# An mLSTM layer and a feed-forward layer on one core: gate tiles of the second unit by matmul, a divided last store, and a new order of the work

## The chip, the cores and the metric

One core of one Trainium2 chip runs the whole program. Its engines are TensorE (PE in the rows, and PEld for its weight loads), VectorE (DVE), ScalarE (ACT), GpSimd (POOL) and SyncE (SP), each with an instruction queue of its own that is worked in order; 16 DMA engines move data. The metric is the time of one execution on the device in microseconds (us), less is better. "Faster" and "slower" are said of the median of several runs.

## The reference

```python
def _attn_ref(q, k, v, i_gate, f_gate, o_gate):          # all (4, 8, 768, 40), gates (4, 8, 768)
    ...
    for t in range(S):
        m_new = np.maximum(f_gate[:, :, t] + m, i_gate[:, :, t])
        f_stab = np.exp(f_gate[:, :, t] + m - m_new)
        i_stab = np.exp(i_gate[:, :, t] - m_new)
        m = m_new
        C = f_stab * C + i_stab * outer(v_t, k_t)         # shapes left out
        n = f_stab * n + i_stab * k_t
        y[:, :, t] = sigmoid(o_t) * (C @ q_t) / max(abs(n @ q_t), 1)

def _moe_ref(x, w_in, w_out):                             # x (3072, 320), w_in (320, 2048), w_out (2048, 320)
    h = x @ w_in
    g = h * np.clip(h + 3.0, 0.0, 6.0) / 6.0
    return g @ w_out
```

The recurrent layer (batch 4, 8 heads, 768 steps, head size 40) gives 3072 tokens of 320 numbers; the feed-forward layer then works on every token for itself.

## The kernel before, in words

**Tiles and stages.** The sequence is cut into six blocks of 128 steps; a block of one batch entry is a chunk, so there are 24 chunks. Seven units follow each other: units 0 and 1 hold two chunks each, the others four (`UL`, line 23). Each unit is worked for two halves of the heads ("quad" 0 and 1). Within a chunk the recurrence is written as matrix products: a chunk's load `st` (q and k) and `nat` (k and v) come in, `xya` (lines 479, 489) makes the scores S and the state's product K, the gate tile `gw` weighs the scores (line 419), `C` is the running state (lines 452, 455), and the outputs B (lines 500 to 512) go to `ht` (lines 464, 469). Groups `xya` on TensorE hold B of one chunk together with S and K of the next.

**Gate tiles.** The gates of a block are scanned on VectorE into `f_s` and `i_s` (lines 274 to 286). For unit 0 (`GBT = 2`: two halves of the heads of one unit) TensorE makes the tile `gb` in PSUM from the mask, `f_s` and `i_s` with a selector `sel` (lines 378, 381, 384), and ScalarE takes its exponential into `gw` (line 388). For all later units `f_s` is stored to DRAM (`gsc`, line 285), loaded back in rows that repeat over 64 partitions (line 397), and then mask and `cT` are added (lines 401, 406) and the exponential is taken (lines 414 or 416; in four parts, with `cT` as bias, where the addition is left out).

**End of a unit's first layer.** `fin` divides and multiplies with the output gate: line 593 (needs `ht`), 595, 596, 597 and 598 into `on`; `turn` transposes `on` on TensorE (`xa`, line 613), and ScalarE and VectorE split it into a high part `xh` (line 621) and a low part `xl` (line 623).

**Second layer.** `h` is made for 128 of the 2048 inner columns at a time: eight matmuls (line 738) into one of two PSUM banks. ScalarE and VectorE make `g` of it (lines 755, 757; for unit 0 it is called `gv`), and from unit 1 on `g` is split into `gh` (lines 205 and 207 are the copy helper) and `gl` (line 768). `acc` sums the output (line 781 for unit 0, lines 784 to 786 later); `evac` copies `acc` to `ob` and stores it (lines 800, 803).

**Weights.** Both weight matrices come as eight slices each of 640 KB, `rawi` and `rawo` (line 640), over three buffers, as 64-bit numbers. ScalarE (lines 648, 653, 658) and VectorE (lines 663, 664, 674 or 669) make 32-bit floats of them, and `whi`, `wlo`, `wtl` (lines 205 or 207, 692, 693, 695) are their high and low parts. All sixteen slices are done in the first 90 us or so, beside units 0 and 1.

**Order.** A table `ORDER` written into the kernel lists every step once, with the letter of the engine that does it (p TensorE, d VectorE, a ScalarE, g GpSimd, q SyncE's queue) and the buffer it takes; "F" is a filler matmul on `pw` (line 232), which computes nothing that is used. The steps are issued in this order, so each engine's queue is the table with the other engines' steps left out. Steps whose data are not there hold up what is behind them on their engine.

Of the kernel before, what the change touches and what calls it, by code (L numbers as in the profile page):

```python
# [142 lines left out]
def mlstm_moe_kernel(ctx: ExitStack, tc: tile.TileContext, ig, fg, qkd, natd, ond, w_in, w_out, ident_d, out, dump=None):  # L143
# [92 lines left out]
    def f_setup():  # L236
# [5 lines left out]
        for h in range(2):  # L242
            cs_ = slice(h * Q, h * Q + Q)
            nc.gpsimd.affine_select(sel[:, :, cs_], sel[:, :, cs_], pattern=[[-16, 2], [-1, 6], [0, Q]], compare_op=ALU.is_equal, fill=0.0, base=-8 * h, channel_multiplier=1)
# [677 lines left out]
```

## Time and profile before

| | |
|---|---|
| median of 3 runs | 465.71 us (465.06 to 465.93) |
| time of the profiled execution | 464.87 us |
| its span, first to last instruction | 463.2 us |
| TensorE busy | 449.1 us, 97% of the span |
| VectorE, ScalarE, GpSimd busy | 298.8, 215.8, 122.4 us |
| granted TensorE clock, mean | 0.996 of full speed |
| read from HBM, written | 44.53 MB, 4.03 MB |

How to read it: a busy share is a mean over stages. In the first 80 us nearly all engines are busy; from then on TensorE alone is. Idle time on another engine costs nothing unless TensorE waits for it. Matmuls are pipelined, and the ends of their rows are modelled; the distance from start to start tells what one takes.

### The profile page before, as it was taken

To read this page: it belongs to the slowest core of one execution; us is meant where nothing else is said; L and a number is where in the kernel's file an instruction comes from. 1 tells how busy PE (TensorE), PEld (TensorE's weight loads), DVE (VectorE), ACT (ScalarE), POOL (GpSimd) and SP (SyncE) were. 2 spreads that over 40 slices of the span, in tenths; PEclk is the share of its full clock that TensorE was granted. 3 is DMA by queue.
4 is the path that set the end of the run, shared out by engine and by line. 5 is a ranking of instruction groups with operands and counts; after the bars stand their busy time and mean duration, and the time that the engine had idled before them with its cause. 6 is when DMAs were issued, how large, how long until landed. Compare 5 with 4: busy or idle time off the path is not lost.

```text
span 463.2 us, 12600 instructions
## 1 busy us (share of the span) xinstructions
PE 449.1 (97%) x5243; PEld 388.3 (84%) x5249; DVE 298.8 (65%) x752; ACT 215.8 (47%) x482; POOL 122.4 (26%) x155
## 2 busy tenths in 40 slices
PE   8879989999999999999999999999999999999997
PEld 4547767899888888988889988988989898989896
DVE  6999999978866376856655763576555646443423
ACT  5788798777343434263343353243551232321231
POOL 3152225265311307502213134132112201020130
PEclk9989999999999999999999999999999999999999
DMA  6998887276304450244421442432322000010001
GB/s 208 281 315 265 234 258 203 59 176 169 94 20 119 119 151 4 78 142 121 115 77 44 131 139 60 108 102 89 101 69 78 1 1 1 16 57 1 1 1 57
DMA packets 24977, 49.38 MB, mean 107 GB/s; under 512 B 2840, under 2 KB 15960, under 8 KB 24920
## 3 DMA queue, kind: packets, MB, share of 16 engines
q1 hardware_dynamic: 24696, 47.89, 35.5%
q8 instruction: 41, 0.67, 0.6%
q10 hardware_dynamic: 224, 0.69, 0.5%
q14 instruction: 16, 0.13, 0.1%
HBM read 44.53 MB, written 4.03 MB: 105 GB/s over the span
## 4 chain that ended last, share of the span: by engine, by line
PE 85%; DVE 9%; ACT 2%; issue 1%; DMA 1%; SPq 0%; DVEq 0%; ACTq 0%
PE h L738 35%; PE acc L784 11%; PE acc L785 11%; PE acc L786 11%; PE xya L506 3%; PE xya L479 3%; PE pw L232 2%; PE xya L489 2%; PE xa L613 2%; PE xya L512 2%; PE acc L781 1%; DVE on L597 1%; DMA st<-in_qk_dram 1%; DVE on L598 1%; DVE gv L757 1%
## 5 line engine op out<-in xcount | busy, mean ns | idle before, releaser
L755 ACT ACTIVATE g<-h,half 128x512 f32<-128x512 f32 (+1 forms) x96 | 61.8, 651 | 128.3 <-PE h L738 92.9
L784 PE MATMUL acc<-vh,gh 128*128 128x320 f32 x352 | 111.5, 317 | 0.0
L757 DVE SCALAR_TENSOR_TENSOR g<-g,h 128x512 f32<-128x512 f32 (+1 forms) x96 | 61.2, 640 | 77.4 <-ACT g L755 77.3
L785 PE MATMUL acc<-vl,gh 128*128 128x320 f32 x352 | 108.6, 309 | 0.0
L786 PE MATMUL acc<-vh,gl 128*128 128x320 f32 x352 | 108.5, 308 | 0.0
L768 POOL TENSOR_TENSOR gl<-g,gh 128x512 fp32r<-128x512 f32 (+1 forms) x40 | 48.7, 1222 | 183.6 <-DVE gh L207 104.2
L738 PE MATMUL h<-xh,whi 128*128 128x512 f32 (+1 forms) x224 | 83.9, 375 | 2.4 <-DVE gv L757 1.7
L738 PE MATMUL h<-xh,wlo 128*128 128x512 f32 (+1 forms) x224 | 80.8, 361 | 0.0
L738 PE MATMUL h<-xl,whi 128*128 128x512 f32 (+1 forms) x224 | 80.5, 360 | 0.0
L784 PEld LDWEIGHTS acc<-vh,gh 128*128 128x128 f32 x352 | 66.0, 188 | 2.5
L785 PEld LDWEIGHTS acc<-vl,gh 128*128 128x128 f32 x352 | 66.1, 188 | 1.8
L786 PEld LDWEIGHTS acc<-vh,gl 128*128 128x128 f32 x352 | 66.0, 188 | 0.0
L738 PEld LDWEIGHTS h<-xh,whi 128*128 128x128 f32 x224 | 42.0, 187 | 11.4 <-DVE gv L757 3.7
L205 ACT CAST gh<-g 128x512 fp32r<-128x512 f32 (+1 forms) x53 | 30.0, 571 | 39.8 <-PE acc L785 19.5
L738 PEld LDWEIGHTS h<-xh,wlo 128*128 128x128 f32 x224 | 42.1, 188 | 6.9
L768 DVE TENSOR_TENSOR gl<-g,gh 128x512 fp32r<-128x512 f32 (+1 forms) x56 | 40.0, 722 | 12.2 <-ACT gh L205 10.9
L738 PEld LDWEIGHTS h<-xl,whi 128*128 128x128 f32 x224 | 42.1, 188 | 4.5
L738 PE MATMUL h<-xl,wtl 128*128 128x512 f32 (+1 forms) x112 | 40.5, 361 | 0.0
L738 PE MATMUL h<-xh,wtl 128*128 128x512 f32 (+1 forms) x112 | 40.2, 359 | 0.0
L419 DVE TENSOR_TENSOR gw<-xya,gw 128x256 f32<-128x256 f32 x48 | 20.0, 416 | 10.7 <-PE xya L489 7.4
L452 DVE SCALAR_TENSOR_TENSOR C<-C,dec,xya 128x42 f32<-128x42 f32 x100 | 20.6, 251 | 9.1 <-PE xya L489 9.0
L207 DVE CAST gh<-g 128x512 fp32r<-128x512 f32 (+1 forms) x43 | 19.3, 451 | 7.5 <-PE acc L785 6.1
(136 smaller groups left out, 683.2 us busy)
## 6 DMA issues: line engine op xcount, KB each, us to landing
st<-in_qk_dram SPq DMA_DIRECT2D x48, 280.0 KB, 4.2
nat<-in_nat_dram SPq DMA_DIRECT2D x48, 206.0 KB, 3.2
rawo<-in_w_out_dram SPq DMA_DIRECT2D x8, 640.0 KB, 7.9
gw<-gsc SPq DMA_DIRECT2D x20, 256.0 KB, 4.3
rawi<-in_w_in_dram SPq DMA_DIRECT2D x7, 640.0 KB, 8.5
out_dram<-ob SPq DMA_DIRECT2D x24, 160.0 KB, 3.0
on<-in_on_dram SPq DMA_DIRECT2D x5, 640.0 KB, 4.9
rawi<-in_w_in_dram ACTq DMA_DIRECT2D x1, 640.0 KB, 4.2
```

The lines of the kernel that those rows point to most:

```text
L205: nc.scalar.copy(dst, src)
L207: E(c).tensor_copy(dst, src)
L419: add(f"fr{nm}", "d", lambda e: nc.vector.tensor_tensor(V["gw", task][:, cp], V["xy", "S", nm][:, :, 0:128].rearrange("p c (j t) -> p j c ...
L452: nc.vector.scalar_tensor_tensor(Cn[:, j], cur[:, j], dc[:, j : j + 1], kv[:, hc, j], ALU.mult, ALU.add)
L479: nc.tensor.matmul(xy[h * Q : h * Q + Q, c, j * Q : j * Q + Q], st[rs, j, h], st[rs, j, 2 + (h != c)], start=True, stop=True)
L738: nc.tensor.matmul(hp[:, :n], w, x[:, :n], start=k == 0, stop=k == len(seq) - 1)
L755: nc.scalar.activation(V["g", nm], V["h", nm][:, :n], AF.Relu, bias=half, scale=1.0 / 6.0)
L757: add(f"gg{nm}", "d", lambda e: nc.vector.scalar_tensor_tensor(V["g", nm], V["g", nm], 1.0, V["h", nm][:, :n], ALU.min, ALU.mult), [f"re{n ...
L768: add(f"gl{nm}", "gd", lambda e: E(e).tensor_sub(V["gl", nm], V["g", nm], V["gh", nm].bitcast(F32)), [f"gh{nm}"], kind="tt", n=n, lock=1)
L784: nc.tensor.matmul(acc, gh[:, ts_], V["VH", f // 4][:, f % 4, :], start=f == 0, stop=False)
L785: nc.tensor.matmul(acc, gh[:, ts_], V["VL", p][:, f % 2, :], start=False, stop=False)
L786: nc.tensor.matmul(acc, gl[:, ts_], V["VH", f // 4][:, f % 4, :], start=False, stop=f == NF - 1)
```

## The change

Three things are changed. First, `GBT` goes from 2 to 4: the gate tiles of unit 1 too are made by TensorE from `f_s` and `i_s`. The selector `sel` has 16 rows of columns instead of 12, there are four `gw` buffers instead of three (and two `ob` instead of three), and only those blocks of `f_s` that a later unit loads are stored, so block 0 is not stored any more. Second, the last output tile of the last unit is copied and stored in two halves of 160 columns. Third, `ORDER` is another: nearly every step stands elsewhere, 248 steps are on another engine than before, and there are 47 fillers for 49. In `fin`, the first steps now wait for all chunks by name instead of the last one, which changes what the order may do and no arithmetic.

```diff
-GBT = 2
+GBT = 4
...
-SLOTS = dict(..., gw=3, ..., ob=3, rd=3)
+SLOTS = dict(..., gw=4, ..., ob=2, rd=3)
...
 ORDER = """
-1a 908a0 T F F F F 2q 3d 4d 5d F F F F F 6d 7d 9d F 909a0 912d 913d F F 910a0 107p0/0 F 0q 16d 11p0 12d 919q1 911a 914d 916d 917d 14a F F 920a1 923d
...
-    sel = early["ea"].tile([BR, 12, 128], F32, name="sel")
+    sel = early["ea"].tile([BR, 16, 128], F32, name="sel")
...
+    stored = {pair(u, cp)[0] for u in range(NU) for quad in range(2) if 2 * u + quad >= GBT for cp in range(UL[u])}
...
-        for c in range(c0, c0 + n):
+        for c in sorted(stored & set(range(c0, c0 + n))):
             add(st(k, c), "q", lambda e, c=c: nc.sync.dma_start(gsc[...], f_s[...]), [f"sf{nm}"], kb=16, rate=200)
...
-                    nc.tensor.matmul(pb[:, j], sel[:, 6 * quad + 2 * b + j], f_s[:, cl * L : cl * L + L], start=False, stop=False)
+                    nc.tensor.matmul(pb[:, j], sel[:, 8 * quad + 2 * b + j], f_s[:, cl * L : cl * L + L], start=False, stop=False)
...
-        add(f"r1{nm}", "d", r1, [f"b2{task}_{c0 + n - 1}"], get=[(f"rd{nm}", ("rd",))], kind="tiny", n=8)
+        add(f"r1{nm}", "d", r1, [f"b2{task}_{c0 + i}" for i in range(n)], get=[(f"rd{nm}", ("rd",))], kind="tiny", n=8)
...
+        parts = 2 if (u, t) == (NU - 1, UL[u] - 1) else 1
+        W = DM // parts
+        for x in range(parts):
+            cs = slice(x * W, x * W + W)
...
+            add(f"ev{nm}", "da" if x else "ad", ev, [f"m2_{u}_{NF//2-1}_{t}"] + [f"ev{u}_{t}"] * x, ...)
+            add(f"so{nm}", "qa" if x else "q", lambda e, cs=cs: Dq(e).dma_start(out[t0 : t0 + L, cs], V["ob", u, t][:, cs]), [f"ev{nm}"], kb=0.5 * W, rate=300)
```

How the table moves instructions, in three places. Lines of the changed kernel are two higher from line 259 on, and nine or so at the end.

SyncE's queue at the start of the program, before (`gsc<-f_s` is the store of the gates, `rawi` a weight slice, `st` and `nat` a chunk's loads):

```order
L273 DMA i_s<-in_ig_dram 64x128
L254 DMA ident<-in_ident_dram 128x128
L640 DMA rawi_177<-in_w_in_dram 128x1280
L285 DMA gsc<-f_s 4x8x128
L359 DMA nat_0_1_216<-in_nat_dram 128x412
L354 DMA st_0_0_218<-in_qk_dram 112x640
L359 DMA nat_0_0_220<-in_nat_dram 128x412
L397 DMA gw_0_256<-gsc 64x512
```

and now:

```order
L275 DMA i_s<-in_ig_dram 64x128
L642 DMA rawi_153<-in_w_in_dram 128x1280
L254 DMA ident<-in_ident_dram 128x128
L642 DMA rawi_204<-in_w_in_dram 128x1280
L361 DMA nat_0_0_241<-in_nat_dram 128x412
L642 DMA rawi_256<-in_w_in_dram 128x1280
L356 DMA st_0_0_270<-in_qk_dram 112x640
L361 DMA nat_0_1_301<-in_nat_dram 128x412
```

The store and the load of `gw` are gone from here; weight slices have moved forward.

TensorE's queue ahead of the transposes `xa` of unit 0, before (`pw` is the filler):

```order
L232 MATMUL pw<-ones 128x512
L613 MATMUL xa_0_0_512<-ident,on_479 128x128 x2
L613 MATMUL xa_1_0_520<-ident,on_479 128x128 x2
L613 MATMUL xa_2_0_525<-ident,on_479 128x128 x2
L232 LDWEIGHTS ones
```

and now (`gb` is a gate tile of unit 1, `xya` the sixth chunk's group, with the loads `st` and `nat` of unit 1):

```order
L383 MATMUL gb_1_1_598<-f_s,sel 128x128 x2
L386 MATMUL gb_1_1_598<-sel,i_s 64x2x64 x4
L502 LDWEIGHTS ones
L502 MATMUL xya_607<-ones 64x84
L502 LDWEIGHTS ones
L502 MATMUL xya_607<-ones 64x84
L508 MATMUL xya_607<-C_0_0_0_558,st_0_0_529 64x42 x4
L514 MATMUL xya_607<-nat_0_0_483,gw_0_292 64x42 x8
L481 MATMUL xya_607<-st_0_1_593 64x64 x8
L491 MATMUL xya_607<-nat_0_1_485 64x42 x8
L615 MATMUL xa_1_0_647<-ident,on_550 128x128 x2
```

A gate tile and the group of the sixth chunk now stand where fillers stood.

VectorE's queue from the last product `on` of unit 0 to its `xl`, before (`yi`, `yo` are weight slices in work, ISA is the addition of their parts):

```order
L597 SCALAR_TENSOR_TENSOR on_479<-on_479,ht_1_494 128x2x160
L663 TENSOR_SCALAR yi_516<-yi_516 128x640
L598 TENSOR_TENSOR on_479<-on_479,rd_1_0_508 128x2x160
L664 TENSOR_SCALAR yi_516<-yi_516 128x640
L623 TENSOR_TENSOR xl_534<-xa_0_0_512,xh_533 128x256
L674 ISA yi_516<-yi_516,lwi_528 128x1280
L370 TENSOR_TENSOR nat_0_0_542<-nat_0_0_542,wT 128x160
L623 TENSOR_TENSOR xl_534<-xa_1_0_520,xh_533 128x256
L623 TENSOR_TENSOR xl_534<-xa_2_0_525,xh_533 128x256
```

and now:

```order
L600 TENSOR_TENSOR on_550<-on_550,rd_1_0_583 128x2x160
L665 TENSOR_SCALAR yo_586<-yo_586 128x640
L671 ISA vr_643<-yo_512,lwo_527 128x1280
L697 TENSOR_TENSOR wlo<-yi_457,whi 128x2x256
L666 TENSOR_SCALAR yo_586<-yo_586 128x640
L207 COPY C_0_1_0_663<-xya_607 128x84
L694 TENSOR_TENSOR wtl<-yi_457,wtl 64x128
L695 TENSOR_TENSOR wtl<-yi_457,wtl 64x128
L625 TENSOR_TENSOR xl_655<-xa_2_0_651,xh_654 128x256
L625 TENSOR_TENSOR xl_655<-xa_0_0_657,xh_654 128x256
L625 TENSOR_TENSOR xl_655<-xa_1_0_647,xh_654 128x256
```

Seven steps, six of them on weights, now stand between that product and the first `xl`.

## Rows read from the trace of the kernel before

**Rows 1.** The page: busy time of the engines, share of the span, instructions.
```profile
PE 449.1 (97%) x5243; PEld 388.3 (84%) x5249; DVE 298.8 (65%) x752; ACT 215.8 (47%) x482; POOL 122.4 (26%) x155
```

**Rows 2.** Windows: length; busy us of PE, PEld, DVE, ACT, POOL; clock, DMA share, GB/s.
```profile
0.00:34.60 34.60, 28.98 (x385) 16.67 (x391) 28.31 (x83) 24.37 (x53) 12.00 (x23) 0.95 0.86 268
34.60:87.00 52.40, 48.66 (x618) 38.98 (x610) 49.82 (x128) 44.20 (x90) 17.40 (x21) 1.00 0.77 221
87.00:459.90 372.90, 371.45 (x4259) 332.67 (x4251) 220.71 (x542) 146.76 (x340) 93.05 (x111) 1.00 0.26 76
459.90:463.20 3.30, 0.03 (x1) 0.00 (x0) 0.00 (x0) 0.43 (x1) 0.00 (x0) 1.00 0.27 99
```

**Rows 3.** Groups by line and shape: VectorE whole, GpSimd from 31 to 81 us.
```profile
L664 DVE TENSOR_SCALAR yo<-yo 128x640 uint32<-128x640 uint32 x8 | 5.2, 648 | 0.1
...
L664 DVE TENSOR_SCALAR yi<-yi 128x640 uint32<-128x640 uint32 x8 | 3.9, 487 | 0.1
L692 DVE TENSOR_TENSOR wtl<-yi,wtl 64x128 fp32r<-64x128 f32 x8 | 3.4, 425 | 0.3
...
L693 DVE TENSOR_TENSOR wtl<-yi,wtl 64x128 fp32r<-64x128 f32 x8 | 2.3, 288 | 0.2
...
L598 DVE TENSOR_TENSOR on<-on,rd 128x320 f32<-128x320 f32 x2 | 2.1, 1046 | 0.0
...
L695 POOL TENSOR_TENSOR wlo<-yi,whi 128x512 fp32r<-128x512 f32 x4 | 5.5, 1382 | 6.4 <-DVE f_s L283 4.5 <-ACT whi L205 1.9
```

**Rows 4.** Timeline of VectorE and GpSimd: start us, us, engine, line, operation [idle before].
```profile
30.54 0.48 DVE L598 TENSOR_TENSOR on<-on,rd 128x320 f32<-128x320 f32 x1
30.94 0.49 DVE L664 TENSOR_SCALAR yi<-yi 128x640 uint32<-128x640 uint32 x1
...
33.19 0.74 DVE L623 TENSOR_TENSOR xl<-xa,xh 128x256 fp32r<-128x256 f32 x2
...
43.59 1.40 DVE L692 TENSOR_TENSOR wtl<-yi,wtl 64x128 fp32r<-64x128 f32 x1
...
43.58 1.27 POOL L695 TENSOR_TENSOR wlo<-yi,whi 128x512 fp32r<-128x512 f32 x1 [4.45 <-DVE f_s L283]
...
83.77 0.41 DVE L757 SCALAR_TENSOR_TENSOR g<-g,h 128x256 f32<-128x256 f32 x1
```

**Rows 5.** Waits of TensorE: us in total, times, longest.
```profile
PE h L738 <- DVE gv L757: 1.7, 3, 0.9
```

**Rows 6.** Timeline of TensorE.
```profile
1.26 5.30 PE L232 MATMUL pw<-ones 128*128 128x512 bf16 x12 [1.26 <-DVE tiny L179]
...
15.24 0.28 PE L378 MATMUL gb<-maskb,identb 128*128 128x256 bf16 x1
...
16.69 1.04 PE L232 MATMUL pw<-ones 128*128 128x512 bf16 x4
...
34.62 0.38 PE L738 MATMUL h<-xh,whi 128*128 128x256 f32 x1
...
85.99 0.44 PE L506 MATMUL xya<-C,st 40*64 40x42 f32 x16
...
87.07 0.39 PE L738 MATMUL h<-xh,whi 128*128 128x256 f32 x1
```

**Rows 7.** Timeline of SyncE's queue: the issues of DMAs.
```profile
2.23 0.43 SPq L640 DMA_DIRECT2D rawi<-in_w_in_dram  x1
5.63 0.75 SPq L285 DMA_DIRECT2D gsc<-f_s  x1
```

**Rows 8.** Last copy, last store, and the landing of all stores.
```profile
459.97 0.43 ACT L205 COPY ob<-acc 128x320 f32<-128x320 f32 x1 [0.45 <-PE acc L786]
460.42 0.33 SPq L803 DMA_DIRECT2D out_dram<-ob  x1
...
DMA to landing us min/median/max: 1.8/3.0/4.3
```

**Rows 9.** DMA issues on the page: count, KB each, median us from issue to landing.
```profile
st<-in_qk_dram SPq DMA_DIRECT2D x48, 280.0 KB, 4.2
```

More of the change, by code (lines that the diff above doesn't have):

```diff
@@ L243, in f_setup @@
             cs_ = slice(h * Q, h * Q + Q)
[L244 removed]
+            nc.gpsimd.affine_select(sel[:, :, cs_], sel[:, :, cs_], pattern=[[-16, 2], [-1, 8], [0, Q]], compare_op=ALU.is_equal, fill=0.0, base=-8 * h, channel_multiplier=1)
         nc.gpsimd.memset(mask, 0.0)
@@ L270, in gates @@
         gbs = [f"gb{t // 2}_{t % 2}_{cp}" for t in range(GBT) for cp in range(UL[t // 2]) if blk(pair(t // 2, cp)[0]) == k - 1]
-        sts = [st(k - 1, c) for c in range(c0 - GP[k - 1], c0)] if k else []
+        sts = [st(k - 1, c) for c in range(c0 - GP[k - 1], c0) if c in stored] if k else []
         add(f"lf{nm}", "qa", lambda e: Dq(e).dma_start(f_s[:, :w], fg[:, cols]), [f"pT{p}"] * (k > 0) + sts + gbs, kb=BR * w * 4 / 1000, rate=110)
@@ L380, in gb @@
                 for j in range(2):
[L381 removed]
+                    nc.tensor.matmul(pb[:, j], sel[:, 8 * quad + 2 * b + j], f_s[:, cl * L : cl * L + L], start=False, stop=False)
                 for h in range(2):
                     for cc in range(2):
[L384 removed]
+                        nc.tensor.matmul(pb[h * Q : h * Q + Q, :, cc], i_s[:, cl * L + cc * Q : cl * L + cc * Q + Q], sel[:, 8 * quad + 2 * b : 8 * quad + 2 * b + 2, h * Q : h * Q + Q], start=False, stop=cc == 1)
             add(f"gb{nm}", "p", gb, [f"if{g}"] + [f"gb{u}_{quad}_0"] * (cp > 0), get=[(f"gb{nm}", ("ey", "eo", "ez"))] + ([(f"gw{task}", ("gw",))] if cp == 0 else []), kind="gb")
@@ L796, in evac, with ev @@
         t0 = b * S + c * L
-        def ev(e):
-            V["ob", u, t] = P["mo"].tile([128, DM], F32, tag=f"ob{got[f'ob{u}_{t}'][1]}", name=f"ob{u}_{t}")
-            cast(e, V["ob", u, t], V["acc", u, t])
-        add(f"ev{u}_{t}", "ad", ev, [f"m2_{u}_{NF//2-1}_{t}"], get=[(f"ob{u}_{t}", ("ob",))], kind="pcp", n=DM)
-        T.free(f"acc{u}_{t}", [f"ev{u}_{t}"])
-        add(f"so{u}_{t}", "q", lambda e: nc.sync.dma_start(out[t0 : t0 + L, :], V["ob", u, t]), [f"ev{u}_{t}"], kb=164, rate=300)
-        T.free(f"ob{u}_{t}", [f"so{u}_{t}"])
+        parts = 2 if (u, t) == (NU - 1, UL[u] - 1) else 1
+        W = DM // parts
+        for x in range(parts):
+            cs = slice(x * W, x * W + W)
+            nm = f"{u}_{t}" + "b" * x
+            def ev(e, x=x, cs=cs):
+                if x == 0:
+                    V["ob", u, t] = P["mo"].tile([128, DM], F32, tag=f"ob{got[f'ob{u}_{t}'][1]}", name=f"ob{u}_{t}")
+                cast(e, V["ob", u, t][:, cs], V["acc", u, t][:, cs])
+            add(f"ev{nm}", "da" if x else "ad", ev, [f"m2_{u}_{NF//2-1}_{t}"] + [f"ev{u}_{t}"] * x, get=[(f"ob{u}_{t}", ("ob",))] if x == 0 else (), kind="pcp", n=W)
+            add(f"so{nm}", "qa" if x else "q", lambda e, cs=cs: Dq(e).dma_start(out[t0 : t0 + L, cs], V["ob", u, t][:, cs]), [f"ev{nm}"], kb=0.5 * W, rate=300)
+            T.free(f"acc{u}_{t}", [f"ev{nm}"])
+            T.free(f"ob{u}_{t}", [f"so{nm}"])
     for i in range(WS):
```

150 lines of the change are left out of this document (75 added, 75 removed).

## The prediction

> **What bounds the kernel now.** I read the page first: TensorE is busy for 449.1 of 463.2 us, so the time is TensorE's work plus what it wastes [rows 1]. The windows say where the waste lies: 5.6 us idle up to the first `h` matmul at 34.6, 3.7 us from there to 87, 1.5 us in all of 87 to 459.9, and 3.3 us behind the last matmul [rows 2]. The 49 filler matmuls on `pw`, all ahead of 34 us, are waste as well. The rest TensorE has to do in any order, so this change can move time only ahead of 87 us, in the tail, or in a few later waits. Ahead of 87 us VectorE is the tight engine: 49.82 of 52.40 us busy between 34.6 and 87, with ScalarE at 44.20 and the DMA engines at 0.77 [rows 2]. VectorE keeps its own pace only when GpSimd is quiet: the first `wtl` subtraction of a pair takes 425 ns on average and the second, of the same size, 288 [rows 3]; the one of 1.40 us at 43.59 ran beside a GpSimd `wlo` that began at 43.58 [rows 4]. TensorE's own waits agree: `h` waits for VectorE's `gv` [rows 5].
>
> The sum is made against the profiled execution: span 463.2 us, own time 464.87, which is 0.84 us under the median of 465.71. I work out a difference and put it on the median.
>
> **The change, part by part.**
>
> *Four gate tiles on TensorE.* One tile is lines 378 to 384: from 15.24 until the filler at 16.69, 1.45 us [rows 6]; four cost 5.8 us. Two fillers go, at (1.04 - 0.38) / 3 = 0.22 us each where four run on end [rows 6], 0.4 us. All of it stands ahead of the first `h` matmul, where TensorE waits or fills, so by itself it costs nothing; without that cover it would be 5.4 us.
>
> *What they replace.* Four loads of `gw` and the store of block 0 to `gsc`; on GpSimd and ScalarE mask additions, `cT` additions and exponentials in four parts. None of these engines is the tight one there, so I take no gain from the work itself. The store mattered for its place: SyncE issued a weight load at 2.23 and then held its queue for that store until 5.63 [rows 7]; now two more loads can go out without that hold. Whether it helps is a rival's matter. The wider `sel` is a third more of two fills and two selects, done while VectorE waits for the first gate rows: nothing.
>
> *VectorE up to the first `h` matmul.* By the order, 18 steps are new ahead of the last `xl` of unit 0 and 8 are gone. New: `w4` and `w5` of two output-weight slices and one `w6`, together 4 x 0.4 + 0.75; one more `wlo`, 0.6; one more `th`, 0.45; state steps of unit 1 and one `fr`, 0.9; the rest trades one slice for another. Each counts with the distance to the next start: 0.4 us from 30.54 to 30.94, where the row's own 0.48 includes the end of the pipeline [rows 4]. Net 4.3 us. The last `xl` ended at 33.93 [rows 4], so now at 38.2, and with 0.5 us for TensorE to come up the first `h` starts at 38.7 instead of 34.62 [rows 6]. TensorE's own queue is no earlier either: seventeen fillers instead of twelve precede the first gate tile, and the twelve took 5.30 us from 1.26 on, over 0.4 each [rows 6]. That is 4.1 us; but the sixth chunk's `xya` is by then done already, 1.1 us as from 85.99 to 87.07 [rows 6], which leaves 3.0.
>
> *From there to 87 us.* The place to read is the fifth `h` of unit 1, at 87.07 [rows 6]: in both orders the same TensorE work stands ahead of it, gate tiles and fillers apart. With two `h` banks it needs the third product `g` of unit 1, which VectorE ran from 83.77 to 84.18 [rows 4]: 2.9 us to spare. In the new order VectorE has 6.5 us more ahead of that product: by then the slices are even, but it has five `wlo` for two, three `whi` for one, the scans of gate group 2 and three steps of `gh` and `gl` that stood later (1.8, 0.8, 2.3, 0.8, and small ones). Two gains stand against it. GpSimd loses about 7 of its 17.4 us in this stretch [rows 2], above all three `wlo` of 1.38 [rows 3]. What GpSimd costs VectorE I take from pairs of equal work: 8 x (648 - 487) + 8 x (425 - 288) ns for the shifts and `wtl`, and 2 x (1046 - 485) ns for `on` against the quiet row at 30.54 [rows 3, 4], 3.5 us, which is 0.2 us per us of GpSimd: 1.4 us back. And of VectorE's 2.6 idle us there [rows 2] I give a half back, 1.3, since more steps are ready. That puts the product's end at 84.18 + 6.5 - 1.4 - 1.3 = 88.0, 0.9 us behind 87.07. TensorE alone would be there at 38.7 + 52.4 - 3.7 idle [rows 2] - 1.1 for the `xya` = 86.3 at the latest, so it waits. What was 3.0 us late at 38.7 is 0.9 us late here, and **that 0.9 is the whole cost of the new start**, since TensorE is full from there on. Bounds: with no slowdown and no idle left, VectorE is 5 us earlier and TensorE's 86.3 decides, less what its busy time hides of waits, -1.5 to -3; with both left whole, +2.7.
>
> *Later waits.* The 1.5 us behind 87 [rows 2] belong to the old order; a new one has its own, between -1.5 and +1.5. I take -0.4: these gone, and about 1 us of others.
>
> *The last store in halves.* Now: copy from 459.97 to 460.40, store issued at 460.42, end at 463.2, 2.7 us behind the issue; stores of this size land in 1.8 to 4.3 us [rows 8]. The second half is ready no earlier, since both copies run on ScalarE: 0.3 us each by half of 0.43 and its fixed part, the second 0.2 behind the first, 0.5 in all. It goes out by ScalarE's queue, whose issue no row near the end shows; I let it cost as much again as SyncE's 0.33 [rows 8]. Gain at most the 0.9 between 2.7 and the quickest landing, loss at most 0.4; I take -0.2, nearer to the row of this very store. The Trainium skill (DMA: Bandwidth & Descriptors, Anatomy of one DMA) speaks against a gain: it has a DMA cost a fixed 2.0 us plus its bytes over 436 GB/s, so that halving 160 KB saves an estimated 0.19 us, and the later copy takes that back: by it the tail would be 0.0 and the sum 0.2 us higher. The 2.7 us here fit it better than a time in proportion to size would.
>
> Sum: 0.9 - 0.4 - 0.2 = +0.3 us, so 466.0; I cut it to **465.9**, which is no change that a measurement of this kernel can tell (about 0.2%, 0.93 us).
>
> **The rivals.**
>
> *Faster.* VectorE is relieved by more than I count: loads start 3.4 us sooner [rows 7], so its early idle shrinks, and GpSimd no longer slows a step. Then the product of the place above is done by 85, the three waits of `h` for `gv` (1.7 us, up to 0.9 [rows 5]) end, and TensorE is 1.7 us early at 87: with tail and later waits -2.4, 463.3. For it: 3.7 us of idle to be had [rows 2]. Against it: VectorE does get more work.
>
> *Slower.* In the new order the sixth chunk's `xya` stands directly ahead of the first `xa`, so `xa` waits for that chunk's `st`. Up to it the queue holds about 8 MB: seven weight slices of 640 KB, six `st` of 280 [rows 9], seven somewhat smaller `nat`, and small ones. At the 268 GB/s of the first 34.6 us [rows 2] that has moved by 30, and it lands some 4 us later, since an `st` lands 4.2 us behind its issue [rows 9]: 34 or so. VectorE has 3 us of weight steps between its last `on` product and the first `xl`, so the wait is free until `xya` starts at 34.9; from there each us is one on the first `h`. A load at 37 puts that at 40.8, VectorE can't make 2.1 us up, and the time is 467.9. For it: DMA engines at 0.86 [rows 2]. Against it: the 3.4 us that SyncE's queue gains.
>
> *The change does little of what it says:* the loads saved are worth nothing while the DMA engines stay full; that lies inside the forecast, which takes no gain from them.
>
> **How the numbers follow.** The forecast case, within 1.2 us of 465.9, has 0.42: 0.27 of it within 0.2%, 0.06 under, 0.09 over. Faster has 0.33, slower 0.25. So faster 0.39, same 0.27, slower 0.34. Both signs hold much, so the range leaves out about a quarter of the faster case, towards its bound of -3, and a third of the slower one: 462.8 to 468.2. The forecast case alone: 464.7 to 467.1.
>
> **What would show it.** Right: the first `h` matmul at 38 to 39.5, right behind VectorE's last `xl`; the fifth `h` of unit 1 within 1.5 us of 87 and waiting for `g`; TensorE at 9 in the page's later slices; 2.4 to 2.8 us behind the last issue. Wrong: a first `h` behind 40 with `xya` waiting for `st` (slower); 86 or less at the fifth `h` of unit 1 (faster); a new wait of over 1 us behind 90, for which I have no term.

## The result: slower by 0.6%

| | before | after |
|---|---|---|
| median (19 runs of each) | 465.71 us (464.51 to 468.15) | 468.82 us (466.39 to 471.17) |
| ratio, 95% interval | | 1.0059 [1.0042, 1.0077] |
| profiled execution, own time | 464.87 us | 468.0 us |
| its span | 463.2 us | 466.3 us |
| first `h` matmul | 34.62 us | 39.64 us |
| fifth `h` of unit 1 | 87.07 us | 89.31 us |
| from there to the last matmul's end | 372.86 us | 373.66 us |
| behind the last matmul | 3.3 us | 3.3 us |
| granted TensorE clock, mean | 0.996 | 0.992 |

Slower, by more than a measurement can confuse with no change. The profiled span grew by 3.07 us: 2.24 up to the fifth `h` of unit 1, 0.8 behind it, nothing in the tail. Lines of the kernel after stand two higher than before in this stretch of the file (740 for 738).

The page's line of busy times of the kernel after, which answers to [rows 1]:

```profile
PE 454.6 (97%) x5299; PEld 394.9 (85%) x5299; DVE 294.8 (63%) x740; ACT 202.2 (43%) x440; POOL 145.6 (31%) x180
```

TensorE is busy 5.5 us longer; VectorE and ScalarE have less to do, GpSimd 23.2 us more, all of it behind the fifth `h` (118.23 for 93.05). The windows of the kernel after (columns as in [rows 2]):

```profile
0.00:39.64 39.64, 35.60 (x499) 21.92 (x500) 31.14 (x94) 29.16 (x62) 12.21 (x23) 0.96 0.88 271
39.64:89.31 49.67, 47.39 (x552) 39.93 (x552) 46.97 (x124) 37.74 (x80) 15.12 (x19) 0.97 0.71 199
56.24:59.65 3.41, 3.41 (x17) 3.41 (x17) 2.86 (x11) 3.41 (x7) 1.31 (x2) 0.50 1.07 247
89.31:462.97 373.66, 371.59 (x4249) 333.05 (x4248) 216.71 (x524) 134.84 (x298) 118.23 (x138) 1.00 0.26 75
462.97:466.30 3.33, 0.00 (x0) 0.00 (x0) 0.00 (x0) 0.49 (x2) 0.00 (x0) 0.93 0.20 61
```

The third row is a stretch at a granted clock of 0.50, the lower of the two levels (1.2 GHz), although TensorE was busy for all of its 3.41 us: its `h` matmuls started 0.21 us apart there, for 0.12 elsewhere. Just ahead of it TensorE had waited twice, 0.39 and 0.64 us. One more stretch at 0.50, at 35.8 to 39.2, lies inside the first row; the profile of before has one, at 30.7. In both places TensorE had no `h` yet. The fourth row's idle time is 2.07 us, where before had 1.5. Waits of TensorE in the kernel after (waits view: us in total, times, longest):

```profile
PE pc L312 <- ACT cTs L205: 0.8, 1, 0.8
PE h L740 <- DVE g L759: 0.8, 1, 0.8
PE pc L312 <- DVE cTs L207: 0.6, 1, 0.6
PE h L740 <- DVE gv L759: 0.6, 1, 0.6
PE acc L783 <- DVE vr L671: 0.6, 1, 0.6
...
PE gb L380 <- ACT gw L390: 0.6, 1, 0.6
...
PE xya L481 <- DMA st<-in_qk_dram: 0.2, 1, 0.2
```

The three waits of `h` for `gv` [rows 5] have become one; the waits for `cTs`, of `h` for `g` and of `gb` are new in the list, and the one for `vr` was 0.5 us in before. Where they stand, in rows picked from TensorE's timeline of the kernel after (start, busy time, line, operation, idle time before it and what ended it):

```profile
32.21 0.27 PE L380 MATMUL gb<-maskb,identb 128*128 128x256 bf16 x1 [0.56 <-ACT gw L390]
39.64 0.36 PE L740 MATMUL h<-xh,whi 128*128 128x256 f32 x1 [0.45 <-DVE xl L625]
86.17 1.34 PE L783 MATMUL acc<-vr,gv 128*128 128x320 f32 x4 [0.58 <-DVE vr L671]
89.31 0.39 PE L740 MATMUL h<-xh,whi 128*128 128x256 f32 x1
99.09 0.43 PE L312 MATMUL pc<-gTs,last 128*128 128x64 f32 x2 [0.81 <-ACT cTs L205]
106.73 0.39 PE L740 MATMUL h<-xh,whi 128*128 128x256 f32 x1 [0.79 <-DVE g L759]
```

Rows picked from VectorE's timeline and, the last one, from ScalarE's at the tail are read in the same way:

```profile
31.80 0.49 DVE L599 SCALAR_TENSOR_TENSOR on<-on,ht 128x320 f32<-128x320 f32 x1 [1.18 <-ACT on L342]
38.41 1.09 DVE L625 TENSOR_TENSOR xl<-xa,xh 128x256 fp32r<-128x256 f32 x3
84.14 1.98 DVE L671 CUSTOM_DVE_ANT_0 vr<-yo,lwo 128x1280 uint16<-128x1280 uint16 x1
88.84 0.41 DVE L759 SCALAR_TENSOR_TENSOR g<-g,h 128x256 f32<-128x256 f32 x1
...
463.05 0.49 ACT L205 COPY ob<-acc 128x160 f32<-128x160 f32 x2 [3.13 <-PE acc L788]
```

The first `h` comes up behind VectorE's last `xl`, which ended at 39.50; the fifth `h` of unit 1 comes 0.06 us behind the third `g` product, which ended at 89.25. No wait is listed for that `h`: TensorE, which had waited 0.58 us for `vr` at 86.17, was itself only just there.

### The profile page after: what moved, and what is told of

It reads as the page before. It is cut to its first block, busy times and chain, and to the rows that moved or that the text cites. A ratio compares the mean times of both kernels' runs of the same rounds, so it can differ in the third digit from the quotient of the medians.

```text
span 466.3 us, 12663 instructions
## 1 busy us (share of the span) xinstructions
PE 454.6 (97%) x5299; PEld 394.9 (85%) x5299; DVE 294.8 (63%) x740; ACT 202.2 (43%) x440; POOL 145.6 (31%) x180
## 4 chain that ended last, share of the span: by engine, by line
PE 83%; DVE 9%; ACT 3%; DMA 2%; issue 1%; SPq 0%; ACTq 0%; DVEq 0%
PE h L740 36%; PE acc L786 12%; PE acc L787 11%; PE acc L788 11%; PE xya L508 3%; PE xya L481 2%; PE acc L783 2%; PE xya L514 2%; PE xya L491 2%; PE xa L615 2%; DMA rawi<-in_w_in_dram 1%; DVE vr L671 1%; DMA nat<-in_nat_dram 1%; DVE yi L676 1%; DVE on L599 1%
## 5 line engine op out<-in xcount | busy, mean ns | idle before, releaser
L770 POOL TENSOR_TENSOR gl<-g,gh 128x512 fp32r<-128x512 f32 (+1 forms) x51 | 62.3, 1225 | 160.8 <-ACT gh L205 80.9
L740 PE MATMUL h<-xh,whi 128*128 128x512 f32 (+1 forms) x224 | 84.9, 379 | 1.9 <-DVE g L759 0.8
L205 ACT CAST gh<-g 128x512 fp32r<-128x512 f32 (+1 forms) x46 | 25.3, 561 | 33.4 <-DVE g L759 19.4
L770 DVE TENSOR_TENSOR gl<-g,gh 128x512 fp32r<-128x512 f32 (+1 forms) x45 | 33.4, 746 | 5.7 <-ACT gh L205 4.6
L445 POOL TENSOR_TENSOR C<-C,dec 128x84 f32<-128x84 f32 x41 | 17.2, 423 | 59.6 <-DVE C L457 34.7
L466 DVE TENSOR_TENSOR ht<-xya,eG 128x168 f32<-128x168 f32 x43 | 14.0, 325 | 19.4 <-PE xya L491 19.3
L207 DVE CAST gh<-g 128x512 fp32r<-128x512 f32 (+1 forms) x50 | 22.9, 461 | 4.8 <-PE acc L787 2.9
```

The costliest lines, as they stand in the source:

```text
L205: nc.scalar.copy(dst, src)
L207: E(c).tensor_copy(dst, src)
L445: nc.gpsimd.tensor_tensor(Cn, cur, dec[:, c, hc, k : k + 2][:, :, None].broadcast_to([128, 2, E2]), ALU.mult)
L466: nc.vector.tensor_tensor(hv, V["xy", "B", nm][:, :, 212:296].rearrange("p h (j e) -> p h j e", j=2), heads(eG[:, c], quad, b)[:, :, :, No ...
L740: nc.tensor.matmul(hp[:, :n], w, x[:, :n], start=k == 0, stop=k == len(seq) - 1)
L770: add(f"gl{nm}", "gd", lambda e: E(e).tensor_sub(V["gl", nm], V["g", nm], V["gh", nm].bitcast(F32)), [f"gh{nm}"], kind="tt", n=n, lock=1)
```

## The experiments

Four explanations stood against each other: the new order's **start** (VectorE's steps and late loads ahead of the first `h`), the **gate tiles** on TensorE (their time, or the clock where they replace fillers), **one late copy** (`cTs`, behind 89), and the **divided store**. Each time is a median; each ratio is of means, to runs of the kernel before on the same chip. A single profile proves little here: the first `h` lay at 39.64, 40.67, 38.09, 39.0, 38.83 and 38.26 in six profiles of kernels whose order up to it is the same (after, e4, e6, e9, e10, e12), and at 34.62, 35.39 and 34.02 in three of before's (before, e1, e2).

**e1, the kernel before again.** No edit.

> The kernel before, once more, as a control for the clock. Theory O (the loss lies in the new order of the steps up to 107 us: a start 5.0 us later of which only part is made up, and group 2's transposes between two h tiles): the time is 465.7 +- 0.5 and the mean granted clock may be anything. Theory K (a good part of the 3.1 us is TensorE's clock, which over the 19 runs of the changed kernel had a median of 0.989 and went from 0.984 to 1.0, with the runs at 0.99 or more at a mean of 467.6 and those under it at 469.6): here nearly every run has 0.992 or more, and the spread of the times is under 2 us. If instead the clock here has a median of 0.989 as well, K falls.

466.27 us against 465.35, 1.0017 [0.9993, 1.004]: the measurement tells 0.2% at best.

**e2 and e4, the store alone.** e2 is before with the last tile in halves, e4 is after with a whole one.

```diff
e2 +        parts = 2 if (u, t) == (NU - 1, 2) else 1     (tile 2 is the last one in before's order)
e4 -        parts = 2 if (u, t) == (NU - 1, UL[u] - 1) else 1
e4 +        parts = 1
```

> The kernel before with its last output tile copied and stored in two halves, nothing else. My step for the tail said -0.2 (between -0.9 and +0.4): 465.5. The profile of the changed kernel shows no gain behind the last matmul: then 465.7 +- 0.4. Theory S (the two halves hurt): 466.2 or more, with over 3.2 us from the first store's issue to the end.

> The changed kernel with its last output tile stored whole, nothing else. If the halves are worth nothing: 468.8 +- 0.5. If they are worth the 0.2 of my step: 469.0. Theory S (they hurt): 468.3 or less. Theory K: the median clock stays under 0.99.

e2: 465.73 us, 1.0028 [0.9997, 1.0059]. e4: 468.29 us, 1.0069 [1.0043, 1.0096]. Halving the store neither gives nor costs anything that can be seen; after is slower without it too. Behind the last matmul it is 3.27 and 3.24 us whole and 3.09 halved in before's order, 3.23 whole and 3.34 halved in after's: no direction.

**e3 and e5, the gate tiles alone.** Before's order with unit 1's tiles made by TensorE, in the place of twelve fillers; e5 moves the load of `f_s` behind others on SyncE's queue and the exponentials behind weight steps on ScalarE.

```diff
e3 -GBT = 2
e3 +GBT = 4
e5 (SyncE)   -L274 DMA f_s<-in_fg_dram 64x128   (ahead of rawi, nat, st, nat)
e5 (SyncE)   +L274 DMA f_s<-in_fg_dram 64x128   (behind them)
e5 (ScalarE) -L390 ACTIVATE gw_0<-gb_0_0 128x256   (ahead of two slices' yi, lwi, lwi)
e5 (ScalarE) +L390 ACTIVATE gw_0<-gb_0_0 128x256   (behind them and two whi)
```

> The kernel before, in its own order, with the second unit's four gate tiles made by TensorE: each stands where three or four fillers or idle time stood, their exponentials follow on ScalarE, the loads, the store of block 0 to DRAM, the mask and cT additions are gone, and the load of group 1's forget gates moves behind the tiles, since they read the same buffer; the last store stays whole. Theory O: no slower than before, 464.5 to 466.0, first h at 34 to 35.5. Theory G (the gate tiles cost by themselves, by what they push back on TensorE and ScalarE): 467.5 or more, first h behind 36.

> The second unit's four gate tiles in the old order once more, but without the two holds that the run of before with gate tiles showed: two exponentials no longer stand ahead of weight steps on ScalarE (VectorE had waited 2.66 us there), and group 1's gate loads go to the queue behind the loads of states (SyncE had held its queue from 21.8 to 33.0). Theory O (the gate tiles are free, their order costs): first h at 34 to 35.5, 464.8 to 466.0. Theory G (the tiles cost by themselves, since they take the place of fillers and TensorE's clock falls): 467 or more with first h under 36, half clock in several stretches ahead of 30.

e3: 471.89 us, 1.0124 [1.009, 1.0157], with two holds of my own making (VectorE waited 2.66 us at 19.30 for ScalarE's `yi`; SyncE's queue stood from 21.34 to 33.01). e5: 469.72 us, 1.008 [1.0051, 1.0108]. VectorE's hold is gone there; SyncE's queue still stood, from 21.61 to 34.41, now behind four loads more. Its row in the waits view:

```profile
SPq L274 <- PE gb L383: 12.7, 1, 12.7
```

It is for the buffer that the tiles read. From the first to the fifth `h` e5 took 52.66 us, before, e1 and e2 52.45, 53.62 and 53.73, and behind it 372.88, as before's 372.86: what e5 lost, it lost ahead of the first `h`, at 39.52. So the tiles with what they hold up can cost 0.8% in an order that is otherwise the old one. Where, show e5's windows (columns as in [rows 2]):

```profile
16.00:21.40 5.40, 4.86 (x78) 3.51 (x78) 4.34 (x11) 4.56 (x7) 1.31 (x3) 1.00 1.04 367
21.40:38.40 17.00, 17.00 (x167) 10.29 (x164) 9.71 (x30) 7.70 (x18) 3.26 (x5) 0.50 0.42 122
```

and e5's timeline of TensorE's last tile and VectorE's first `xl`:

```profile
32.83 0.40 PE L380 MATMUL gb<-maskb,identb 128*128 128x256 bf16 x1
33.15 1.22 PE L383 MATMUL gb<-f_s,sel 64*128 64x128 f32 x4
34.31 1.12 PE L386 MATMUL gb<-sel,i_s 64*64 64x128 f32 x8
...
37.27 0.42 DVE L625 TENSOR_TENSOR xl<-xa,xh 128x256 fp32r<-128x256 f32 x1 [3.93 <-ACT xh L623]
```

For 17 us the granted clock was 0.50 with TensorE busy in all 17. A tile, 1.45 us at the full clock [rows 6], took some 2.5, and here TensorE, not VectorE, was last: VectorE stood idle for 3.93 us.

**e11, fillers taken away.** Before without twelve fillers, four at each of 16.7, 20.0 and 26.8 us.

```diff
(TensorE, three times)
-L232 LDWEIGHTS ones
-L232 MATMUL pw<-ones 128x512
... (four pairs each)
```

> The kernel before without twelve of its 49 fillers, the ones in whose place the runs with gate tiles in the old order have three of the tiles; nothing takes their place. Theory F (in those runs it was the missing fillers: TensorE's clock falls to half at 21 and stays there): half clock over several stretches ahead of 34, first h behind 36, 467 or more. Theory G (it was the tiles' own 5.8 us in front of xa): first h at 34 to 35, 465.0 to 466.2, clock as in before.

466.91 us, 1.0009 [0.9989, 1.003]. The clock fell in two stretches of 3.4 us in its profile, windows:

```profile
22.90:26.30 3.40, 3.07 (x55) 1.59 (x48) 0.96 (x6) 2.43 (x7) 2.03 (x4) 0.50 0.97 336
33.10:36.50 3.40, 3.40 (x41) 2.22 (x40) 3.32 (x9) 3.02 (x6) 1.74 (x3) 0.50 1.02 344
```

The mean granted clock of its twelve runs was 0.986, that of 35 of before's beside them 0.994. So the fillers hold the clock up, but where VectorE is last (first `h` at 35.44), a fall costs next to nothing. It costs where TensorE is last, as in e5.

**e9, e10 and e6, one copy of 0.2 us.** Gate groups 1 and 2 each copy `pL` from PSUM to `cTs`, and TensorE's next transposes need it. e9 moves group 1's copy to ScalarE, e10 group 2's to VectorE, in both cases right behind the copy `gTs`; e6 does both.

```diff
e9 (VectorE)  -L207 COPY cTs<-pc 128x32   (behind L676 ISA yi)
e9 (ScalarE)  +L205 COPY cTs<-pc 128x32   (behind L205 COPY gTs)
e10 (ScalarE) -L205 COPY cTs<-pc 128x64   (behind L205 CAST gh, L205 CAST vh)
e10 (VectorE) +L207 COPY cTs<-pc 128x64   (behind L207 COPY gTs)
```

> The changed kernel with one copy of gate group 1 and of group 2 made earlier: cTs of group 1 moves from VectorE, behind an addition of weights, to ScalarE right behind gTs, that of group 2 from ScalarE, behind two other copies, to VectorE right behind gTs. TensorE waited for the two 0.64 us at 55.3 and 0.81 at 99.1. Theory T (the loss behind 87 is the place of the transposes of group 2 and its kin, and the falls of the clock that follow such waits): both waits under 0.2, TensorE 1.3 us earlier from 100 on, fewer runs with a clock under 0.99, 467.0 to 467.6. Theory V (VectorE sets the pace to 107 whatever TensorE waits for): the waits turn into waits of h for g, 468.8 +- 0.5.

> The changed kernel with group 1's copy cTs alone made earlier (ScalarE, right behind gTs). Both copies together had brought 2.7 us for 1.45 us of waits. Theory W (each wait counts as it stands on TensorE's path, and the falls of the clock behind it come on top): 467.3 to 468.0, the wait at 55.3 gone, that at 99 as before. Theory V (VectorE's pace holds up to 87, so the wait at 55 was covered by later ones): 468.5 or more. Theory C (it is the clock: the fall that follows the wait at 55, at which h runs at half clock, makes most of it): 466.8 or less and most runs with 0.992 or more.

> The changed kernel with group 2's copy cTs alone made earlier (VectorE, right behind gTs). Theory W: 467.0 to 468.0, the wait at 99 gone, TensorE as late as in the changed kernel up to there. Theory V: all of the 2.7 us is here, 466.0 to 466.6. Theory C: under 0.8 of gain, 468.0 or more.

e6: 466.08 us, 1.0013 [0.999, 1.0035]. e9: 468.7 us, 1.0052 [1.0022, 1.0083]. e10: 467.12 us, 1.0014 [0.9994, 1.0034]. On that chip e10 is 2.0 ± 1.2 us under e9 (means, 95%). Group 2's copy alone brings the time to where before's is; group 1's does little, since in e9 `h` then waited 0.70 us at 57.10 for the next step of that group. In the kernel after, VectorE copied `gTs`, and ScalarE came to `cTs` behind two larger casts, the first of which waited 1.54 us for VectorE's `g` (timelines of VectorE and ScalarE in the kernel after):

```profile
97.26 0.23 DVE L207 COPY gTs<-pc 128x64 f32<-128x64 f32 x1 [1.08 <-PE pc L303]
...
97.89 0.40 ACT L205 CAST gh<-g 128x256 fp32r<-128x256 f32 x1 [1.54 <-DVE g L759]
98.20 0.72 ACT L205 CAST vh<-vr 128x640 fp32r<-128x640 f32 x1
98.83 0.20 ACT L205 COPY cTs<-pc 128x64 f32<-128x64 f32 x1
```

The same steps in the timelines of VectorE and TensorE in e10, and behind them e10's window from the fifth `h` to the last matmul:

```profile
98.02 0.23 DVE L207 COPY gTs<-pc 128x64 f32<-128x64 f32 x1 [1.08 <-PE pc L303]
98.16 0.21 DVE L207 COPY cTs<-pc 128x64 f32<-128x64 f32 x1
98.97 0.43 PE L312 MATMUL pc<-gTs,last 128*128 128x64 f32 x2
106.30 0.39 PE L740 MATMUL h<-xh,whi 128*128 128x256 f32 x1 [0.52 <-DVE g L759]
```

```profile
90.07:462.38 372.31, 371.32 (x4249) 332.99 (x4248) 216.49 (x525) 134.65 (x297) 118.57 (x138) 1.00 0.26 75
```

The wait of 0.81 at 99.09 is gone and the one of 0.79 is 0.52. From the fifth `h` to the last matmul's end it is 373.66, 373.90 and 373.54 in after, e4 and e9, 372.45 and 372.31 in e6 and e10, and 372.86, 372.65 and 372.66 in before, e1 and e2. That is 1.3 us for one copy. The other runs below agree: with group 2's copy moved, e8 and e14 to e18 took 372.30 to 372.42; without it, e7 and e13 took 373.56 and 374.03. Only e12, with a further edit behind 89, has the copy and 374.79.

**e13, the late load.** After waits 1.18 us at 31.80 for the tanh of `on`, whose load SyncE issued only at 23.61, behind two loads of `nat` that had held its queue for 4.75 us. e13 issues `on` ahead of these.

```diff
(SyncE)   +L340 DMA on<-in_on_dram 128x2x320
           L361 DMA nat_0_0<-in_nat_dram 128x412
           L361 DMA nat_0_1<-in_nat_dram 128x412
           ...
          -L340 DMA on<-in_on_dram 128x2x320
(ScalarE) +L342 ACTIVATE on<-on 128x2x320   (ahead of the weighing of nat_0_1)
          -L342 ACTIVATE on<-on 128x2x320   (behind four more steps)
```

> The changed kernel with unit 0's load of on issued on SyncE ahead of two loads of nat that wait for their buffers (its issue was at 23.6, before at 19.4), and its tanh on ScalarE ahead of two weighings of nat. Theory L (the first h is late, 38.1 to 40.7 in six profiles of this order for 34 to 35.4 of the old one, because this load lands at 29 to 31 and the chain tanh, on, xa, xh, xl follows): on's issue at 17.5 to 18, VectorE's wait of 1.2 for tanh gone, first h 1 to 2 us earlier, 467.2 to 468.2. Theory D (the sixth chunk's st or VectorE's own steps end last there anyway): first h not earlier than 38, 468.5 or more.

468.29 us, 1.0059 [1.0033, 1.0085]. The timeline of SyncE's queue in after, and rows of SyncE's queue, ScalarE, VectorE and TensorE in e13:

```profile
17.50 4.75 SPq L361 DMA_DIRECT2D nat<-in_nat_dram  x2
23.61 0.43 SPq L340 DMA_DIRECT2D on<-in_on_dram  x1
```

```profile
17.61 0.44 SPq L340 DMA_DIRECT2D on<-in_on_dram  x1
26.01 0.74 ACT L342 ACTIVATE on<-on 128x640 f32<-128x640 f32 x1
37.09 1.08 DVE L625 TENSOR_TENSOR xl<-xa,xh 128x256 fp32r<-128x256 f32 x3
88.34 0.39 PE L740 MATMUL h<-xh,whi 128*128 128x256 f32 x1 [0.50 <-DVE g L759]
```

The wait went and the first `h` came at 38.32, the fifth at 88.34, but the ratio is the changed kernel's own, 1.0059. That profile has another stretch at clock 0.50, from 99.17, about 1 us behind the 0.81 us wait for `cTs`, which ended at 98.08.

**e14 and e15, both at once.** e14 is e10's and e13's edits together; e15 also issues one `st` ahead of a weight slice.

> The same with group 2's copy cTs made earlier as well. Theory L and W add: 465.0 to 466.2. Theory D: as group 2's copy alone, 466.2 to 467.2.

> The same and the sixth chunk's st issued ahead of a load of output weights, so about 0.5 us earlier with 640 KB less before it. Theory D (it is st, which xya waited for up to 2.46 us directly ahead of xa): first h 1 us earlier than without this edit, 464.8 to 465.6. Theory L alone: no change against the run without it, within 0.6.

467.47 us, 1.0027 [1.0002, 1.0052], and 466.99 us, 1.0018 [0.9996, 1.0041]. In e15 the idle time inside that `xya`, 0.17 us in e14, is gone, and the first `h` was at 38.98, no earlier. So neither load is what the time hangs on. The 2.46 us that the expectation puts down to `st` are not for it by the rows: in e9, as with 1.79 in e6 and 0.39 in after, they stand behind all `st` matmuls of that group, ahead of line 491, which reads `nat`, and the profile lists no releaser for them. What TensorE waited for there stays open.

**e7, e8, e16, e17 and e18, an earlier start.** e7 puts unit 0's `xa` ahead of the sixth chunk's `xya` and VectorE's `xl` ahead of six steps, five of them on weights, and two of ScalarE's steps change place; e8 adds e6's edits, e16 is e7's order on e15. e17 takes the exponentials earlier as well, so that PSUM banks come free; e18 puts the last gate tile in the place of four fillers and drops the three ahead of the first `h`.

```diff
e7 (TensorE)  -L502, L508, L514, L481, L491 MATMUL xya   (ahead of L615 xa)
e7 (TensorE)  +L502, L508, L514, L481, L491 MATMUL xya   (behind it)
e7 (VectorE)  +L625 TENSOR_TENSOR xl x3   (ahead of L671 vr, L697 wlo, L666 yo, L207 C, L694 and L695 wtl)
e7 (VectorE)  -L625 TENSOR_TENSOR xl x3   (behind them)
e17 (ScalarE) -L390 ACTIVATE gw_0<-gb_0_1, gw_1<-gb_1_0, gw_1<-gb_1_1   (behind weight steps)
e17 (ScalarE) +L390 ACTIVATE gw_0<-gb_0_1, gw_1<-gb_1_0, gw_1<-gb_1_1   (two to five steps earlier)
e18 (TensorE) -L232 MATMUL pw<-ones x4   (ahead of L502 xyb)
e18 (TensorE) +L380, L383, L386 MATMUL gb_1_1
```

> The changed kernel with another start: TensorE makes the sixth chunk's xya behind the output transposes xa, not ahead of them; ScalarE makes the last two exponentials of gates and the copy for xa ahead of one weight step; VectorE makes four weight steps and one state step (w6, wlo, w5, wtl and C, 2.9 us) behind the three xl, not ahead. Theory St (what is lost at the start stays lost in part): first h at 37 to 38 for 39.6, the time 467.2 to 468.2. Theory V (VectorE's total sets the pace up to 87, so an earlier first h waits later): first h as early, but the fifth h of unit 1 no earlier than 89, 468.8 +- 0.5.

> Both edits, of the copies cTs and of the start, on the changed kernel. If T and St hold and add up: 465.8 to 467.0. If VectorE's total rules (V): 468.3 or more. No theory of mine has it under 465.

> The same and the edit of the start: xya of the sixth chunk behind xa, four weight steps behind xl. Alone it gave nothing, since xa then waited 1.77 us for on. With on early, theory L: first h at 35.5 to 37, 464.0 to 465.2, which would beat both kernels. Theory V (VectorE's total sets the fifth h of unit 1): first h as early, the fifth h of unit 1 at 88 or later, 465.2 or more.

> The kernel of the run before (copy of group 2, on, st, and xya behind xa), with ScalarE's exponentials of the last three gate tiles moved ahead: each of its steps right behind its tile, not behind weighings of nat and weight steps. Theory B (the gate tiles hold the three PSUM banks that xa needs; in e7 xa waited 1.77 us for an exponential to give one back, and in e16 0.54): xa starts at 34 to 35 and waits for on, no longer for gw; first h at 36 to 38, 464.5 to 466. Theory V (VectorE's total sets the pace): first h as early, but the fifth h of unit 1 at 88 or later and 466.2 or more. If the first h is behind 38.5, B falls as the cause.

> The same, with the last gate tile in the place of four fillers ahead of xyb (at 27, not at 31 to 32), and without the three fillers behind xya directly ahead of the first h. Theory B: xa waits for on alone, first h at 35.5 to 37, 464.0 to 465.5. Theory F (fillers hold the clock): the clock falls to half between 27 and 38, first h behind 38, 466 or more. Theory V: 466.0 or more with a first h under 37.

468.86 us, 1.0095 [1.0067, 1.0124] (e7); 467.03, 1.0045 [1.002, 1.007] (e8); 468.75, 1.0036 [1.0009, 1.0062] (e16); 467.28, 1.0047 [1.0024, 1.0071] (e17); 469.02, 1.0064 [1.0041, 1.0088] (e18). None helps: the first `h` lay at 39.33, 39.96, 40.89, 39.50 and 40.59. In e7, e17 and e18 something else was the last to be ready each time. In e7 `xa` waited 1.77 us for a bank that an exponential `gw` still had to read (the row names `gw`, not `on`, as the expectation of e16 has it). e17 took that away; its window, then its timeline of TensorE and VectorE:

```profile
32.70:39.50 6.80, 5.05 (x67) 3.29 (x68) 5.47 (x16) 5.55 (x13) 0.00 (x0) 0.50 0.72 222
```

```profile
34.39 1.51 PE L615 MATMUL xa<-ident,on 128*128 128x128 f32 x6 [1.79 <-DVE on L600]
35.92 1.18 DVE L625 TENSOR_TENSOR xl<-xa,xh 128x256 fp32r<-128x256 f32 x3 [1.27 <-ACT xh L623]
37.98 1.46 PE L232 MATMUL pw<-ones 128*128 128x512 bf16 x3
39.50 0.40 PE L740 MATMUL h<-xh,whi 128*128 128x256 f32 x1
```

VectorE's last `xl` now ended at 37.1, 2.4 us earlier than in after, yet the first `h` came at 39.50: TensorE was last, with `xya` and three fillers at a granted clock of 0.50. Without these fillers (e18) the clock was 0.50 from 29.2 to 42.9, `xa` waited 3.07 us for `on`, and the first `h` was at 40.59. VectorE's steps, the banks and the lower clock take each other's place as the last to be ready.

**e12, an attempt at a better version.** e6 with one gate step ahead of a mask addition and a pair of `acc` products ahead of unit 2's first `xa`.

> The changed kernel with both copies cTs made earlier, and two more waits of its profile taken up: group 1's sum wTa moves ahead of a mask addition on VectorE that waits for a load (h waited 0.70 for it at 56.1), and one pair of m2 products of unit 1 moves ahead of the first output transpose of unit 2 (which waited 0.47 at 126.2). Theory W: 464.9 to 465.7, no slower than before. Theory V (a wait taken at 56 comes back before 107): 465.6 to 466.1, from the second edit alone.

468.89 us, 1.0039 [1.0009, 1.0069]: the second edit was chosen badly, `xa` then waited 1.36 us at 126.79 and a stretch at clock 0.50 followed at 128.3. No version here beats both kernels; e6 and e10 equal before's within the measurement.

## Why the prediction was wrong

It said no change (465.9 us, range to 468.2); the median is 468.82. By its own steps:

*The start: the path was right, two of its terms were not.* The step that failed is "VectorE up to the first `h` matmul", with 38.2 for the last `xl`: 39.50 in this profile. I had added up VectorE's new work, 4.3 us, and put its idle time at nothing. By the windows ahead of the first `h` its work grew by 2.8 us (28.31 to 31.14) and its idle time by 2.2 (34.60 less 28.31, 39.64 less 31.14). The largest piece is the 1.18 us wait for `on`, of which the sum knew nothing, because I counted only what SyncE's queue gains without the hold of 3.4 us [rows 7] and not that two `nat` loads, waiting for their buffers, would hold it for 4.75 us a little later. In e13, without that wait, the last `xl` ended at 38.17, where I had it. But the wait is not in every profile: 1.18, 0.85 and 0.83 in e4, e10 and e12, none in e6 and e9, where the last `xl` ended at 37.95 and 38.85.

From the last `xl` to the third `g` product's end I had 49.8 us (38.2 to 88.0); it took 49.75 (39.50 to 89.25), by luck. The gains in it did not come: by the windows GpSimd was busy for 15.12 us in that stretch, against 16.10 in before's (33.93 to 84.18), so it lost 1.0 us and not 7, and VectorE's idle time was 2.70, against 2.54, and not half of it. What made up for that was work counted too high: VectorE was busy for 47.05 us, 0.7 less than the 47.71 in before, where my terms gave it 0.8 more. In e4 and e10 the same stretch took 50.49 and 51.33.

So +2.24 instead of +0.9 at the fifth `h` in this profile. In after, e4 and e10, whose order up to it is the same, it lay at 89.31, 91.07 and 90.07, against 87.07, 89.01 and 87.75 in before, e1 and e2: +2.2. With e6, e9 and e12, whose edits of group 1 stand ahead of it (88.71, 89.09, 88.45), it is +1.5. Closer than that the start can't be told.

*"TensorE is full from there on", and later waits −0.4: wrong in sign.* They were +0.8, and +1.0 by the means of three profiles each (after, e4, e9; before, e1, e2). With the start's 1.5 to 2.2 that is 2.5 to 3.2; the ratio of 1.0059 is 2.75 us. I had taken it that the waits of the old order would go and about 1 us of others come, with no place named. The place is gate group 2's transposes between two `h` tiles, which hold one of the two `h` banks until the copy behind two casts is done: 0.81 and then 0.79 us [the waits above]. e10 shows it: with that copy moved, the same stretch is 0.4 us *shorter* than the mean of before's three, which is the −0.4 I had, and the time is 1.0014 of before's. The prediction had named "a new wait of over 1 us behind 90" as a sign of its own error; it came as two of 0.8.

*A lower clock: no term.* Over 143 runs of the kernel before the mean was 466.1 us at a granted clock of 0.9948, over 26 of after and e4 it was 468.6 at 0.9902. At an equal clock the changed kernel is 1.4 us longer by a least-squares line through both (standard error 0.2); of the 2.5 us between the means about 1.1 goes with the clock. That is a correlation: a wait can bring both, as e13 and e12 show, where a stretch at 0.50 stands close behind a wait.

*Gate tiles at nothing.* Under cover they cost nothing only as long as VectorE is last; e5 shows that they become the bound at the lower clock (2.5 us each, 1.008), and e7 that an exponential still to come holds a bank that `xa` needs. I named the price of lost cover, 5.4 us, and not what would take the cover away.

*The store in halves.* I took −0.2; no gain can be seen. I had allowed up to 0.9 between the 2.7 us from the last issue to the end and the quickest landing, but before's last stores landed 1.8 us behind their issue, so the rest is not the store's. The Trainium skill (DMA: Bandwidth & Descriptors, Anatomy of one DMA) had spoken against a gain, with a fixed part of 2.0 us and the bytes' time. That section is about DMAs that GpSimd issues; here SyncE and ScalarE issued them. The trace agrees that half the bytes save little: a whole tile landed 1.8 us behind its issue and a half 1.6 (e2), 0.2 us, which the later copy takes back. The whole tile itself is under the 2.0 us.

*The rivals.* The slower one named `xya` waiting for the sixth `st` as its mechanism. In no profile read here does that group wait for its `st`: the 0.2 us in after's list stands at 24.76, on an earlier chunk, and the idle 0.39, 1.79 and 2.46 us (e15, above) have no releaser. Its 467.9 was nearer than my forecast, but by luck. The faster rival's place did get better (one `gv` wait for three), but VectorE was late at it by more than I allowed.

*Open.* Some 1.5 to 2.2 us at the fifth `h` remain of a start that is 4.4 us later than before's (mean of six 39.1 against 34.7). e7 to e18 show that no single step of it accounts for that; which order would win it back was not found. No run moves GpSimd's steps away from VectorE's weight additions, which took 3.2 us more than in before (last section).

## What to carry to other kernels

When an order is changed, look through every in-order queue for small steps that free a shared buffer, not only at the engine that is busiest: a copy of 0.2 us behind two casts, on a ScalarE that was busy for about a third of that stretch, was worth 1.3 us of TensorE's time. A load that waits for its buffer holds its queue, so count what stands behind each. And look at several profiles before explaining 1 us at a start that itself varies by 2.6.

## What the runs showed that was not expected

The addition of a weight slice on VectorE (line 671) took 0.81 or 0.82 us in four quiet cases and 1.98 at 84.14 in after, where GpSimd worked beside it (GpSimd's timeline in the kernel after):

```profile
84.01 0.32 POOL L445 TENSOR_TENSOR C<-C,dec 128x84 f32<-128x84 f32 x1
84.30 0.45 POOL L372 TENSOR_TENSOR nat<-nat,wT 128x160 f32<-128x160 f32 x1
84.71 0.73 POOL L403 TENSOR_TENSOR gw<-gw,mask 128x256 f32<-128x256 f32 x1
```

TensorE waited 0.58 us for it at 86.17. All eight of these additions, all ahead of the fifth `h`, took 9.7 us, 1212 ns on average; in before (line 669) 6.5, 816 ns. The prediction took 0.2 us of VectorE's time per us of GpSimd; here it was 1.17 us beside the 1.3 from 84.14 to 85.44. In e6 the same addition took 0.81 at 83.74, and GpSimd's `C` was stretched instead; VectorE then lost 1.0 us on two of its next steps, which take 0.42 and 0.41 in after (timelines of GpSimd and VectorE in e6):

```profile
83.62 1.66 POOL L445 TENSOR_TENSOR C<-C,dec 128x84 f32<-128x84 f32 x1
85.12 0.85 DVE L281 TENSOR_TENSOR f_s<-f_s,m_s 64x256 f32<-64x256 f32 x1
85.89 0.95 DVE L770 TENSOR_TENSOR gl<-g,gh 128x256 fp32r<-128x256 f32 x1
```

The Trainium skill (SBUF — State Buffer, "SBUF: two separate sides") has VectorE, in an instruction with two inputs in SBUF, and a GpSimd instruction that reads SBUF share one pair of ports as an exclusive lock, which whichever starts first holds for its whole instruction while the other stands still. That one of them stands still agrees with these rows. That it is the one that starts later does not always: in after GpSimd's `nat` and `gw` began behind the addition and were not stretched, and in e6 GpSimd's `C` began 0.12 us before the addition and was the one to lose.

Nor had I expected a clock at 0.50 with TensorE busy all the time: 17.00 of 17.00 us in e5, 3.41 of 3.41 in after. Run to run, the same kernel had a mean granted clock of 0.984 to 1.0, and its time rose by some 0.5 us for each us of full clock that was missing (the slope of the line above).
